# Starting bytes of SBUF tiles in a fused attention and gated feed-forward kernel: two unused stretches of 192 bytes

## The chip, the cores and the metric
One core of a Trainium2 chip runs the whole problem in one launch. The metric is the device time of that launch in microseconds, the median of several runs. The engines are named as in the profile: PE is TensorE's matmul, PEld its weight load, DVE is VectorE, ACT ScalarE, POOL GpSimd, and SP the queue that issues the DMAs.

## What is computed
```python
# batch 8, 12 heads, sequence 448, head dimension 64
scores = cap * np.tanh(q @ k.T / sqrt(64) / cap)
attn = softmax(scores)                      # exp, sum, divide
x = (attn @ v)                              # heads joined: 8 x 448 x 768
h = np.maximum(x @ w_in, 0.0)               # 768 -> 1024
u, v = h[..., :512], h[..., 512:]
v_n = (v - mean(v)) / np.sqrt(var(v) + 1e-06)
v_s = einsum('ts,bsd->btd', w_spatial, v_n) + b_spatial[None, :, None]
out = (u * v_s) @ w_out                     # 512 -> 768, float32
```

## The kernel before, in words
The kernel works through eight batches. For every batch three groups of four heads pass through attention: the scores (line 592, fp32, four 64 x 64 quadrants of the array, stationary and moving operand both from `raw`), tanh on ScalarE (line 596), exp on ScalarE (line 603), the product with the values (line 613, `v` stationary, the exponentials `tp` moving), and on VectorE folds over the exponentials for maximum and sum (line 631, tile `red`). The first three groups sum on TensorE instead, with a tile of ones (line 660, `one`). The normalised result is written as `xg`: a rounded high part of 448 columns, a low remainder of 448 columns, and a copy of some columns for one short block.

Then comes the mixture (the function `moe`), all in fp32r with operands split into a high and a low part, so that a product takes three matmuls: high by high, high by low, low by high. Its four products are
- u: lines 749 to 751, `wi1_h` or `wi1_l` stationary (128 columns of it), `xg` moving, 448 columns; 4 groups of 6 x 3 matmuls in a batch;
- v: lines 771 to 776, `xg` stationary, `wi2_h` or `wi2_l` moving, 512 columns; three groups of 6 x 3 and one of 6 x 2 in a batch;
- the spatial product: lines 840 to 845, `vh` or `vl` stationary, `ws_h` or `ws_l` moving, 448 columns; 4 groups of 11 in a batch;
- the output product: lines 865 to 867, `wo_h` or `wo_l` stationary, `xg` (now the gated product) moving, 448 columns; 6 groups of 4 x 3 in a batch.

A planner in the kernel orders all work beforehand: every task has an engine, a fixed cost and a key, and the planner plays the engines through and writes the instructions out in the order that it finds. The tiles' addresses don't enter it. Semaphore waits follow from the tiles that tasks share.

The tiles of SBUF lie one behind the other in each partition, in the order in which pools and tiles are made. Nearly all are a multiple of 256 bytes wide, so they keep the starting byte modulo 256 of what lies ahead of them. The exceptions before are `capt` (128 bytes), `one` (64 columns of use in a tile of 96, 384 bytes) and three tiles `lst` of 12 columns, which take 64 bytes each. So, modulo 256 bytes, there start
- at 0: `raw`, `wi2`, `ws`, `red`, `sh`, `st`, `wi1`, `wo`, `dt`, `one`;
- at 128, behind `one`: `v`, `tp`, `xf`, `rr`, `xg`, `u`, `stg`;
- at 64, behind the three `lst`: `vh`, `vl`, `o` and the staging tiles of the weights.

The slices that the matmuls read start at multiples of 256 bytes within their tiles, so an operand starts where its tile does.

Of the kernel before, what the change touches and what calls it, by code (L numbers as in the profile page):

```python
# [9 lines left out]
F32 = mybir.dt.float32  # L10
# [6 lines left out]
B, H, S, D = 8, 12, 448, 64  # L17
# [256 lines left out]
def attn_moe(ctx, tc, bounded, shared, qk, v, qk2, v2, cap, w_in, w_sp, w_out, out):  # L274
# [5 lines left out]
    def pool(name, bufs, space=None):  # L280
        kw = {"space": space} if space else {}
        return ctx.enter_context(tc.tile_pool(name=name, bufs=bufs, **kw))

    const = pool("const", 1)
# [27 lines left out]
    def weights(name, parts, width):  # L312
        return [const.tile([128, parts, width], F32R, name=f"{name}_{p}") for p in "hl"]
# [3 lines left out]
    if bounded:  # L317

        def keep(tag, n, width, fill=None):
            own[tag] = [const.tile([128, width], F32, name=f"{tag}{i}") for i in range(n)]  # L320
            for t in own[tag]:
                if fill is not None:
                    nc.gpsimd.memset(t, fill)

        keep("red", RED, 2 * PW)
        keep("sh", DEN, 64, 1.0)
        keep("st", DEN, 64, 1.0)
    wi1_h, wi1_l = weights("wi1", NP, FH)
    wo_h, wo_l = weights("wo", 4, DM)
    if bounded:  # L330
        keep("dt", DEN, 64, 1.0)
        one = const.tile([128, D + 32], F32, name="one")[:, :D]
        nc.gpsimd.memset(one, 1.0)

    if not bounded:
# [554 lines left out]
def either(ctx: ExitStack, tc: tile.TileContext, *args):  # L890
# [24 lines left out]
    with tc.If(bits <= CAP_BITS) as cmp:  # L915
        with ExitStack() as es:
            attn_moe(es, tc, True, shared, *args)
    with cmp.Else():
        with ExitStack() as es:
            attn_moe(es, tc, False, shared, *args)  # L920
# [29 lines left out]
```

## Time and profile before

| | |
|---|---|
| median of 3 runs | 736.54 us (735.54 to 736.76) |
| profiled execution, time | 735.65 us |
| profiled execution, span from first to last instruction | 733.8 us |
| granted TensorE clock, mean over the span | 0.992 |
| busy: TensorE, VectorE, ScalarE, GpSimd | 98%, 82%, 65%, 11% of the span |

The profile is of one execution. Its time lies 1.85 us above its span. TensorE's busy time counts a matmul from its start to a modelled end, and matmuls overlap in it, so the pace of a run of matmuls is read from the distances of their starts.

### The profile page before, as it was taken

To read this page: it belongs to the slowest core of one execution; us is meant where nothing else is said; L and a number is where in the kernel's file an instruction comes from. 1 tells how busy PE (TensorE), PEld (TensorE's weight loads), DVE (VectorE), ACT (ScalarE), POOL (GpSimd) and SP (SyncE) were. 2 spreads that over 40 slices of the span, in tenths; PEclk is the share of its full clock that TensorE was granted. 3 is DMA by queue.
4 is the path that set the end of the run, shared out by engine and by line. 5 is a ranking of instruction groups with operands and counts; after the bars stand their busy time and mean duration, and the time that the engine had idled before them with its cause. 6 is when DMAs were issued, how large, how long until landed. Compare 5 with 4: busy or idle time off the path is not lost.

```text
span 733.8 us, 12258 instructions
## 1 busy us (share of the span) xinstructions
PE 718.4 (98%) x4902; PEld 488.2 (67%) x4902; DVE 601.6 (82%) x849; ACT 480.0 (65%) x648; POOL 80.9 (11%) x71
## 2 busy tenths in 40 slices
PE   8996999999999999999999999999999999999997
PEld 3332676575668656786558688568565865698896
DVE  4899999999999989948999996299799688982520
ACT  6999657849784884649875833785876678324321
POOL 2234411600110001000120001000020000200100
PEclk9998999999999999999999999999999999999999
DMA  8565314424221441033330420213321131102002
GB/s 278 163 207 157 111 35 139 161 93 143 69 77 50 132 122 50 26 102 101 101 87 22 155 92 26 63 63 129 101 76 41 60 116 38 52 17 86 1 1 80
DMA packets 34263, 66.50 MB, mean 91 GB/s; under 512 B 6034, under 2 KB 21908, under 8 KB 34196
## 3 DMA queue, kind: packets, MB, share of 16 engines
q1 hardware_dynamic: 34196, 65.62, 28.1%
q8 instruction: 40, 0.66, 0.4%
q14 instruction: 27, 0.22, 0.1%
HBM read 54.40 MB, written 11.18 MB: 89 GB/s over the span
## 4 chain that ended last, share of the span: by engine, by line
PE 88%; DVE 5%; ACT 2%; DMA 2%; issue 1%; SPq 1%; POOL 0%; DVEq 0%; ACTq 0%
PE ps_s L592 15%; PE ps_x L613 15%; PE ps_acc L749 5%; PE ps_acc L750 5%; PE ps_acc L751 5%; PE ps_acc L865 5%; PE ps_acc L866 5%; PE ps_acc L867 5%; PE ps_acc L774 4%; PE ps_acc L776 4%; PE ps_acc L775 4%; PE ps_acc L843 2%; PE ps_acc L844 2%; PE ps_acc L845 2%; DVE red L631 2%; PE ps_acc L771 2%
## 5 line engine op out<-in xcount | busy, mean ns | idle before, releaser
L596 ACT ACTIVATE tp<-ps_s,capt 128x896 f32<-128x896 f32 x168 | 162.5, 1005 | 29.7 <-PE ps_s L592 22.2
L631 DVE TENSOR_TENSOR red<-red,tp 128x1792 f32<-128x1792 f32 x90 | 140.9, 1566 | 23.4 <-ACT tp L603 21.7
L603 ACT ACTIVATE tp<-tp,capt 128x1792 f32<-128x1792 f32 (+1 forms) x96 | 154.1, 1607 | 1.5
L592 PE MATMUL ps_s<-raw 64*64 64x448 f32 x1344 | 146.9, 545 | 3.5 <-ACT tp L596 3.3
L613 PE MATMUL ps_x<-tp,v 64*64 64x448 f32 x1344 | 140.0, 536 | 0.5 <-ACT tp L603 0.4
L631 DVE TENSOR_TENSOR red<-tp 128x1792 f32<-128x1792 f32 x45 | 91.2, 2027 | 13.8 <-ACT tp L603 12.9
L613 PEld LDWEIGHTS ps_x<-tp,v 64*64 64x64 f32 x1344 | 51.2, 133 | 75.9 <-issue 68.7
L592 PEld LDWEIGHTS ps_s<-raw 64*64 64x64 f32 x1344 | 47.4, 133 | 79.3 <-issue 47.5
L798 POOL TENSOR_TENSOR lst<-lst,capt 128x1 f32<-128x1 f32 x32 | 35.0, 1095 | 532.1 <-DVE lst L796 532.0
L749 PE MATMUL ps_acc<-xg,wi_h 128*128 128x448 f32 x180 | 67.5, 375 | 3.1 <-ACT xg L353 3.1
L750 PE MATMUL ps_acc<-xg,wi_h 128*128 128x448 f32 x180 | 66.8, 371 | 0.4 <-DVE xg L349 0.4
L751 PE MATMUL ps_acc<-xg,wi_l 128*128 128x448 f32 x180 | 66.4, 369 | 0.0
L865 PE MATMUL ps_acc<-xg,wo_h 128*128 128x448 f32 x176 | 65.1, 370 | 0.0
L866 PE MATMUL ps_acc<-xg,wo_h 128*128 128x448 f32 x176 | 64.5, 367 | 0.6 <-DVE xg L349 0.6
L867 PE MATMUL ps_acc<-xg,wo_l 128*128 128x448 f32 x176 | 64.4, 366 | 0.0
L353 ACT CAST xg<-o 128x448 fp32r<-128x448 f32 x32 | 18.1, 567 | 53.3 <-DVE o L850 47.8
L774 PE MATMUL ps_acc<-wi_h,xg 128*128 128x512 f32 x126 | 50.6, 402 | 0.0
L639 DVE STREAM_TRANSPOSE red<-red 128x896 f32<-128x896 f32 x45 | 49.6, 1102 | 0.7
L776 PE MATMUL ps_acc<-wi_h,xg 128*128 128x512 f32 x126 | 49.7, 395 | 0.0
L775 PE MATMUL ps_acc<-wi_l,xg 128*128 128x512 f32 x126 | 49.7, 394 | 0.0
L641 DVE TENSOR_REDUCE st<-red 128x28 f32<-128x896 f32 x45 | 48.6, 1079 | 0.7
L631 DVE TENSOR_TENSOR red<-red 128x896 f32<-128x896 f32 x45 | 48.6, 1081 | 0.6
(144 smaller groups left out, 1112.3 us busy)
## 6 DMA issues: line engine op xcount, KB each, us to landing
raw<-in_qk SPq DMA_DIRECT2D x48, 448.0 KB
rr<-rd SPq DMA_DIRECT2D x48, 224.0 KB
out<-o SPq DMA_DIRECT2D x48, 224.0 KB
w<-in_w_in SPq DMA_DIRECT2D x12, 512.0 KB
v<-in_v SPq DMA_DIRECT2D x24, 256.0 KB
v<-in_v SPq DMA_DIRECT2D x24, 192.0 KB
xg<-in_w_out SPq DMA_DIRECT2D x12, 256.0 KB
rd<-dt SPq DMA_DIRECT2D x48, 3.5 KB
```

The lines of the kernel that those rows point to most:

```text
L592: nc.tensor.matmul(ps.t[c * D:(c + 1) * D, e, :S], lhsT=f(raw[c].t)[r, k:k + D], rhs=f(raw[c].t)[r, :S], start=True, stop=True)
L596: th = add("A", act(PW, 1), kk("th", i), lambda ps=ps, tp=tp, o=o: nc.scalar.activation(out=tp.t[:, o:o + PW].rearrange("p (e q) -> p e q" ...
L603: ex = add("A", act_s(w, 1), kk("ex", i), lambda tp=tp, w=w: nc.scalar.activation(out=tp.t[:, :w], in_=tp.t[:, :w], func=AF.Exp, scale=ca) ...
L613: nc.tensor.matmul(x.t[e * D:(e + 1) * D, c, :S], lhsT=vts[g // 2].t[c * D:(c + 1) * D, (4 * (g % 2) + 2 * j + e) * D:(4 * (g % 2) + 2 * j ...
L631: nc.vector.tensor_tensor(o_(), i0(), i1(), op=op)
L749: nc.tensor.matmul(ps, lhsT=wi1_h[:, c, fs], rhs=x[:, XH:], start=(c == 0), stop=False)
L750: nc.tensor.matmul(ps, lhsT=wi1_h[:, c, fs], rhs=x[:, :S], start=False, stop=False)
L751: nc.tensor.matmul(ps, lhsT=wi1_l[:, c, fs], rhs=x[:, XH:], start=False, stop=(c == NP - 1))
L774: nc.tensor.matmul(ps, lhsT=x[:, XH:][:, ts], rhs=wi2_h[:, c], start=(c == 0), stop=False)
L865: nc.tensor.matmul(ps, lhsT=wo_h[:, c, ns], rhs=g[:, XH:], start=(c == 0), stop=False)
L866: nc.tensor.matmul(ps, lhsT=wo_h[:, c, ns], rhs=g[:, :S], start=False, stop=False)
L867: nc.tensor.matmul(ps, lhsT=wo_l[:, c, ns], rhs=g[:, XH:], start=False, stop=(c == 3))
```

## The change
It adds one tile of 48 columns (192 bytes) that nothing reads or writes, between the small tiles and the weights of the first product's u half, and it widens the unused part of the tile `one` from 32 columns to 80, which is 192 bytes more.

```diff
         keep("red", RED, 2 * PW)
         keep("sh", DEN, 64, 1.0)
         keep("st", DEN, 64, 1.0)
+    if bounded:
+        const.tile([128, 48], F32, name="gap")
     wi1_h, wi1_l = weights("wi1", NP, FH)
     wo_h, wo_l = weights("wo", 4, DM)
     if bounded:
         keep("dt", DEN, 64, 1.0)
-        one = const.tile([128, D + 32], F32, name="one")[:, :D]
+        one = const.tile([128, D + 80], F32, name="one")[:, :D]
         nc.gpsimd.memset(one, 1.0)
```

Modulo 256 bytes, `wi1`, `wo`, `dt` and `one` start at 192 afterwards, the tiles behind `one` at 0 (192 + 576 = 768), and `vh`, `vl`, `o` and the staging tiles at 192. `raw`, `wi2`, `ws`, `red`, `sh` and `st` stay at 0.

## Rows read from the trace of the kernel before

**Rows 1.** Page, part 1: busy us (share of the span) xinstructions
```profile
PE 718.4 (98%) x4902; PEld 488.2 (67%) x4902; DVE 601.6 (82%) x849; ACT 480.0 (65%) x648; POOL 80.9 (11%) x71
```

**Rows 2.** Page, part 4: the chain that ended last, by engine
```profile
PE 88%; DVE 5%; ACT 2%; DMA 2%; issue 1%; SPq 1%; POOL 0%; DVEq 0%; ACTq 0%
```

**Rows 3.** Two windows: start:end, length, each engine's busy us, clock, DMA, GB/s
```profile
62.00:77.04 15.04, 8.64 (x44) 4.60 (x37) 14.43 (x26) 14.36 (x24) 3.73 (x4) 0.66 0.50 163
77.04:728.64 651.60, 650.84 (x4302) 461.34 (x4300) 538.82 (x756) 410.69 (x566) 55.16 (x45) 1.00 0.25 78
```

**Rows 4.** Timeline of PE at granted clock 0.5: start us, us
```profile
74.34 0.57 PE L750 MATMUL ps_acc<-xg,wi_h 128*128 128x448 f32 x1
...
75.46 0.57 PE L750 MATMUL ps_acc<-xg,wi_h 128*128 128x448 f32 x1
```

**Rows 5.** Timeline, last batch: output product, then v, then u
```profile
660.22 0.36 PE L865 MATMUL ps_acc<-xg,wo_h 128*128 128x448 f32 x1
...
674.70 0.36 PE L867 MATMUL ps_acc<-xg,wo_l 128*128 128x448 f32 x1
674.89 0.39 PE L774 MATMUL ps_s<-wi_h,xg 128*128 128x512 f32 x1
...
690.00 0.40 PE L772 MATMUL ps_acc<-wi_l,xg 128*128 128x512 f32 x1
...
690.23 0.37 PE L749 MATMUL ps_acc<-xg,wi_h 128*128 128x448 f32 x1
690.23 0.19 PEld L750 LDWEIGHTS ps_acc<-xg,wi_h 128*128 128x128 f32 x1
```

**Rows 6.** Timeline, last batch: u, then the spatial product, then the output
```profile
709.14 0.36 PE L751 MATMUL ps_acc<-xg,wi_l 128*128 128x448 f32 x1
709.34 0.37 PE L843 MATMUL ps_s<-ws_h,vh 128*128 128x448 f32 x1
...
713.60 0.37 PE L841 MATMUL ps_s<-ws_h,vl 128*128 128x448 f32 x1
713.80 0.36 PE L865 MATMUL ps_x<-xg,wo_h 128*128 128x448 f32 x1
```

**Rows 7.** Lines by tile: duration ns min/median/max, first and last start
```profile
L867 PE MATMUL ps_acc<-xg,wo_l x176: 358/367/373, 148.1 to 720.9; 128*128 128x448 f32 x176
L775 PE MATMUL ps_acc<-wi_l,xg x126: 387/393/404, 90.9 to 627.0; 128*128 128x512 f32 x126
...
L844 PE MATMUL ps_acc<-ws_l,vh x87: 360/367/370, 106.2 to 704.9; 128*128 128x448 f32 x87
```

**Rows 8.** Timeline, first seam from u to the spatial product
```profile
122.61 0.36 PE L751 MATMUL ps_acc<-xg,wi_l 128*128 128x448 f32 x1
122.81 0.37 PE L843 MATMUL ps_acc<-ws_h,vh 128*128 128x448 f32 x1
```

**Rows 9.** Timeline, first seam from the spatial product to u
```profile
118.95 0.37 PE L841 MATMUL ps_acc<-ws_h,vl 128*128 128x448 f32 x1
119.15 0.36 PE L749 MATMUL ps_acc<-xg,wi_h 128*128 128x448 f32 x1
```

**Rows 10.** Timeline, first seam from v to u
```profile
196.29 0.40 PE L772 MATMUL ps_acc<-wi_l,xg 128*128 128x512 f32 x1
196.52 0.37 PE L749 MATMUL ps_acc<-xg,wi_h 128*128 128x448 f32 x1
```

**Rows 11.** Scores and value product by line: duration ns min/median/max
```profile
L592 PE MATMUL ps_s<-raw x1344: 536/536/971, 6.5 to 634.5; 64*64 64x448 f32 x192
...
L613 PE MATMUL ps_x<-tp,v x1344: 536/536/587, 13.8 to 639.7; 64*64 64x448 f32 x192
```

**Rows 12.** Groups by form on DVE: busy us, mean ns, idle before
```profile
L631 DVE TENSOR_TENSOR red<-tp 128x1792 f32<-128x1792 f32 x45 | 91.2, 2027 | 13.8 <-ACT tp L603 12.9
L631 DVE TENSOR_TENSOR red<-red,tp 128x1792 f32<-128x1792 f32 x45 | 90.9, 2020 | 15.2 <-ACT tp L603 14.7
```

**Rows 13.** Who waited for rr: us, times
```profile
  DVE xf L696: 0.4, 1
```

## Prediction

> **What bounds the kernel now.** I read the page's busy times first: TensorE is busy 98% of the span [rows 1]. The chain that ended last agrees: TensorE has 88% of it, VectorE 5%, DMA 2% [rows 2]. Two windows then tell where the other engines matter. From 62.00 to 77.04 us TensorE works 8.64 of 15.04 us while VectorE and ScalarE are busy almost throughout; from 77.04 to 728.64 it works 650.84 of 651.60 us [rows 3]. The granted clock is 1.00 in this second window and 0.66 in the first. So after 77 us TensorE's own stream alone sets the end, VectorE has 113 us to spare there, and a nanosecond per matmul is a nanosecond of the kernel times its count.
>
> Next I asked whether the matmuls themselves run at the pace of their columns, because after 77 us an address can move the end only through them. I counted from start to start. While the granted clock was 0.5, the fp32r matmuls of 448 columns started every 0.373 us (74.34 to 75.46 in three steps, [rows 4]), which is 448 columns at 1.2 GHz with nothing left over. At full speed the same columns would take 186.7 ns at 2.4 GHz, but a run of the output product takes 14.48 us for 71 intervals (660.22 to 674.70), 203.9 ns each [rows 5]. The product v with 512 columns (213.3 ns at 2.4 GHz) takes 15.11 us for 65 (674.89 to 690.00), 232.5 ns [rows 5]; the mean over all its runs is 232.6. The spatial product takes 4.26 us for 21 (709.34 to 713.60, [rows 6]); over its 322 intervals inside such runs the mean is 202.6 ns. The surplus over the columns is 17.2, 19.3 and 15.9 ns. By count of the loops there are 576 matmuls of the first product's u half and 576 of the output product (both 448 columns, call them u/o), 528 of v and 352 of the spatial product (g). The pot that an address could change is therefore 1152 x 17.2 + 528 x 19.3 + 352 x 15.9 = 19.8 + 10.2 + 5.6 = 35.6 us, 4.8% of the time.
>
> The surplus isn't even. In one line the lengths run from 358 to 373 ns in u/o, from 387 to 404 in v, from 360 to 370 in g [rows 7]; these ends are modelled and lie some 162 ns above the interval to the next start (the median 367 of L867 against 203.9). Within a run the intervals repeat in a short fixed cycle. So a state is carried from one matmul to the next, and a run settles into one of the cycles that its addresses allow.
>
> **The change part by part.** No instruction is added, removed or reordered: the order of work comes from the planner's fixed costs, and the two stretches hold no data. No queue, wait or transfer changes. What moves are starting bytes within a partition.
>
> I take the starting byte of the moving operand less that of the stationary operand loaded beside it, modulo 256. The load of the next weights starts with each matmul (both at 690.23, [rows 5]) and takes 0.19 us of its 0.20, so the two reads run together. From the tile sizes this difference is, before and after: u/o 128 (x at 128, wi1 and wo at 0), then 64 (x at 0, weights at 192); v 128 (wi2 at 0 moving, x at 128 stationary), then 0; g 192 (ws at 0, vh and vl at 64), then 64 (vh and vl at 192). The attention products keep theirs: scores read raw twice, and tp and v move together.
>
> The new differences 64 and 0 don't occur inside any run of before, but they occur at its seams, where one product hands over to the next.
> - Difference 64: last u matmul (x at 128) against the first g weights (vh at 64). 21 seams, 0.20 us at the first [rows 8] and at the last (709.14 to 709.34, [rows 6]), mean 203.1 ns.
> - Difference 0 with 448 columns: last g matmul (ws at 0) against wi1 or wo at 0. 22 seams, 0.20 us at the first [rows 9] and at the last (713.60 to 713.80, [rows 6]), mean 204.9 ns. Another kind, x moving against x stationary from u or o to v, has 6 seams, 0.19 us at the last (674.70 to 674.89, [rows 5]), mean 199.7.
> - Difference 0 with 512 columns: last v matmul (wi2 at 0) against wi1 at 0. 6 seams, 0.23 us at the first [rows 10] and at the last (690.00 to 690.23, [rows 5]), mean 232.5 ns.
>
> The sum: u/o 1152 x (203.1 - 203.9) = -0.9 us; v 528 x (232.5 - 232.6) = -0.1 us; g 352 x (203.1 - 202.6) = +0.2 us. Together about -0.8 us. A seam is one interval, entered from a state that another difference left, and a long run may settle elsewhere. The bounds from both sides are the shortest and longest lengths of each product [rows 7] held throughout, against the 366, 394 and 365 ns that belong to the mean intervals: u/o -8 to +7 ns, v -7 to +10, g -5 to +5, so -9.2 - 3.7 - 1.8 = -14.7 us and +8.1 + 5.3 + 1.8 = +15.2 us. I take the seam values, because the mean over states has stayed within 199.7 to 204.9 ns at 448 columns at all four differences, while the extremes are single members of a cycle. An uncertainty of 2 ns on u/o, 2 on v and 2 on g is 2.3, 1.1 and 0.7 us.
>
> The rest I cost at nothing. The absolute start seems to do nothing by itself: scores at byte 0 and the value product at byte 128 both have a median of 536 ns [rows 11]. VectorE's folds change from tp at 128 and red at 0 to both at 0; the first fold reads tp twice and the second red and tp, and they take 2027 and 2020 ns [rows 12], so 7 ns x 45 = 0.3 us bounds it, beside TensorE's work; without that cover it would be 0.3 us. The transfers land at other bytes (v and rr at 0 instead of 128), and VectorE waited for rr only 0.4 us, once [rows 13]; if that cover were gone, it would be that 0.4 us.
>
> [...]
>
> The profiled execution took 735.65 us, 0.89 below the median of the runs, 736.54; the sum applies to either: 734.9 and 735.7.
>
> **The rivals.** A difference of 0.2% is 1.47 us here, about what a measurement of this kernel can tell from no change.
>
> Faster: the collisions of u/o thin out at difference 64. It decides from -1.3 ns per u/o matmul (1.47 us / 1152) on. For it: g, already at another difference, is the fastest of the three at 202.6, and the shortest u/o lengths are 8 ns below the mean. Against: the 21 seams average only 0.8 ns less. Half the way to the shortest, -4 ns, gives -4.6 us and 731.9; all the way 727.3.
>
> Slower: in v, moving and stationary operands now start at the same byte, so each load begins in step with the stream that it runs beside, and v settles in its long intervals. It decides from +2.8 ns per v matmul (1.47 / 528); half the way to the longest, +5 ns, gives +2.6 us and 739.2, all the way 741.8. For it: the 22 seams with difference 0 are the slowest kind, 204.9. Against: the six with v's own width are at 232.5, and 199.7 was seen too.
>
> Nothing at all: only something finer than 64 bytes matters, and the time stays at 736.5. The lengths of u/o reach from 358 to 373 ns and those of g only from 360 to 370 [rows 7] at equal columns, which speaks against it; but the two products differ in more than their starts. [...]
>
> **How the numbers follow.** Little change by the sum above: 0.36, nothing at all 0.10, faster 0.32, slower 0.22. The first is likeliest: 735.7 us, with its own range of 735.1 to 738.0. For the range I go to the half-way prices on both sides, 731.9 and 739.2, and a little beyond for the settling that can't be read from seams: 731.5 to 740.0. That leaves about one in ten on either side. Faster by over 0.2% is 0.32, within it 0.46, slower 0.22.
>
> **What would show it.** In the changed kernel the same window from 77 us should still hold TensorE without gaps; the u/o runs should start every 203 ns, v's every 232 to 233, g's every 203, and the chain should be as before. If u/o runs fall below 201 the faster rival is right; if v runs rise above 236 the slower one. If all three cycles are unchanged to the nanosecond, 64 bytes don't matter. The prediction is wrong if seams don't stand for runs, if VectorE's folds change by more than 10 ns, or if the stretch before 77 us moves.

## The result, and the profile after

The changed kernel takes 728.75 us (median of 4 runs, 728.26 to 730.34) against 736.65 us of before in the same comparison: a ratio of 0.9898 with a 95% interval of 0.9878 to 0.9918, 1.0% faster. Forecast were 735.7 us and a range of 731.5 to 740.0; the measured time lies below both.

The page of the changed kernel, busy times and the chain by engine, to set beside [rows 1, 2]:

```profile
PE 711.1 (98%) x4902; PEld 486.6 (67%) x4902; DVE 600.7 (83%) x849; ACT 479.9 (66%) x648; POOL 80.3 (11%) x71
PE 85%; DVE 8%; ACT 2%; DMA 2%; issue 1%; SPq 1%; POOL 0%; DVEq 0%; ACTq 0%
```

TensorE's busy time is 7.3 us shorter with the same 4902 matmuls, the other engines' times change by at most 1.6 us, and the span (726.5 us) is 7.3 us shorter. The chain was forecast to stay as before and doesn't quite: TensorE has 85% of it instead of 88, VectorE 8% instead of 5. Windows of the changed kernel, cut at the corresponding instants (the columns of [rows 3]):

```profile
62.00:76.36 14.36, 8.08 (x39) 4.26 (x32) 13.74 (x25) 13.69 (x24) 3.23 (x4) 0.76 0.52 171
76.36:721.33 644.97, 644.04 (x4302) 460.68 (x4301) 537.94 (x757) 410.95 (x566) 55.20 (x45) 1.00 0.25 78
```

The second window held 651.60 us before and holds 644.97 now, with the same 4302 matmuls and hardly more idle time of TensorE (0.93 us, 0.76 before): 6.6 of the 7.3 us lie here, in the pace of the matmuls. The timeline of PE in the last batches, g, then the output product, then v, then u (start us, length us):

```profile
649.77 0.36 PE L845 MATMUL ps_acc<-ws_h,vh 128*128 128x448 f32 x1
...
653.98 0.36 PE L843 MATMUL ps_acc<-ws_h,vl 128*128 128x448 f32 x1
654.18 0.36 PE L867 MATMUL ps_acc<-xg,wo_h 128*128 128x448 f32 x1
...
668.38 0.36 PE L869 MATMUL ps_acc<-xg,wo_l 128*128 128x448 f32 x1
668.58 0.39 PE L776 MATMUL ps_s<-wi_h,xg 128*128 128x512 f32 x1
...
683.32 0.39 PE L774 MATMUL ps_acc<-wi_l,xg 128*128 128x512 f32 x1
683.54 0.36 PE L751 MATMUL ps_acc<-xg,wi_h 128*128 128x448 f32 x1
```

The 71 intervals of the output product take 14.20 us, 200.0 ns each, where [rows 5] had 14.48 us and 203.9; v's 65 take 14.74 us, 226.8 ns, where it had 15.11 and 232.5; g's 21 take 4.21 us, 200.5 ns, where [rows 6] had 4.26. Over all runs the means are 200.05 (u/o), 227.4 (v) and 200.6 ns (g), against 203.7, 232.6 and 202.6. (The 203.9 is the output product's; the u half had 203.5.) By the starts in the trace the intervals of the output product repeated 203, 212, 200, 209 and 196 ns before and repeat 202, 201 and 197 now: the run has settled into another cycle. The spread within a line has shrunk as well (duration ns min/median/max, as in [rows 7]):

```profile
L869 PE MATMUL ps_acc<-xg,wo_l x176: 360/362/368, 147.2 to 713.8; 128*128 128x448 f32 x176
L777 PE MATMUL ps_acc<-wi_l,xg x126: 389/389/402, 90.3 to 621.4; 128*128 128x512 f32 x126
L846 PE MATMUL ps_acc<-ws_l,vh x87: 360/360/367, 105.3 to 697.9; 128*128 128x448 f32 x87
```

So the shortest length didn't get shorter (358 before, 360 now; the ends are modelled); the long ones are gone. Between starts, the output product's intervals ran from 195 to 212 ns before and run from 197 to 206 now.

What VectorE and ScalarE do meanwhile doesn't set this pace. Two windows of the kernel before (the columns of [rows 3]) lie in runs of the output product:

```profile
155.00:163.00 8.00, 8.00 (x41) 7.36 (x40) 7.93 (x9) 4.98 (x6) 0.00 (x0) 1.00 0.25 92
714.00:728.00 14.00, 14.00 (x70) 12.89 (x69) 1.25 (x2) 3.23 (x6) 0.00 (x0) 1.00 0.20 76
```

VectorE is busy 7.93 of 8.00 us in the first and 1.25 of 14.00 in the second, ScalarE 4.98 and 3.23, and the two runs have 203.8 and 203.9 ns between starts. The DMA engines' share is much the same in both (0.25 and 0.20), so these windows say nothing of transfers.

What was costed at nothing stayed so. The attention products and VectorE's folds, from the lines' durations and the groups by form, beside [rows 11, 12]:

```profile
L594 PE MATMUL ps_s<-raw x1344: 536/536/951, 6.2 to 628.7; 64*64 64x448 f32 x192
...
L615 PE MATMUL ps_x<-tp,v x1344: 536/536/587, 13.5 to 634.0; 64*64 64x448 f32 x192
```

```profile
L633 DVE TENSOR_TENSOR red<-tp 128x1792 f32<-128x1792 f32 x45 | 91.2, 2027 | 13.2 <-ACT tp L605 12.3
L633 DVE TENSOR_TENSOR red<-red,tp 128x1792 f32<-128x1792 f32 x45 | 90.9, 2019 | 14.4 <-ACT tp L605 13.9
```

The starts account for the gain. From the 601st matmul (76.58 us before, 76.12 after) to the last, the intervals inside u/o runs sum to 3.94 us less, inside v runs to 2.62 less, inside g runs to 0.62 less, and where products or kinds of work change to 0.10 less; those inside the attention products sum to 0.43 more. That is 6.85 us, and the first 600 matmuls give 0.46. Most of the 0.43 us is one wait that the faster stream runs into: the timeline (in brackets the idle time and what ended it) shows the weight load of the scores waiting 0.90 us for ScalarE, where it waited 0.58 us before.

```profile
136.73 1.01 ACT L598 ACTIVATE tp<-ps_s,capt 128x896 f32<-128x896 f32 x1
...
137.79 0.21 PEld L594 LDWEIGHTS ps_s<-raw 64*64 64x64 f32 x8 [0.90 <-ACT tp L598]
```

The same load in the kernel before:

```profile
138.60 0.21 PEld L592 LDWEIGHTS ps_s<-raw 64*64 64x64 f32 x8 [0.58 <-ACT tp L596]
```

### The profile page after: what moved, and what is told of

Read it like the earlier page. It is cut to its first block, busy times and chain, and to the rows that moved or that the text cites. A ratio compares the mean times of both kernels' runs of the same rounds, so it can differ in the third digit from the quotient of the medians.

```text
span 726.5 us, 12258 instructions
## 1 busy us (share of the span) xinstructions
PE 711.1 (98%) x4902; PEld 486.6 (67%) x4902; DVE 600.7 (83%) x849; ACT 479.9 (66%) x648; POOL 80.3 (11%) x71
## 4 chain that ended last, share of the span: by engine, by line
PE 85%; DVE 8%; ACT 2%; DMA 2%; issue 1%; SPq 1%; POOL 0%; DVEq 0%; ACTq 0%
PE ps_s L594 14%; PE ps_x L615 14%; PE ps_acc L751 5%; PE ps_acc L867 5%; PE ps_acc L752 5%; PE ps_acc L868 5%; PE ps_acc L753 5%; PE ps_acc L869 5%; PE ps_acc L776 4%; PE ps_acc L777 4%; PE ps_acc L778 4%; DVE red L633 3%; PE ps_acc L845 2%; PE ps_acc L847 2%; PE ps_acc L846 2%; PE ps_acc L773 1%
## 5 line engine op out<-in xcount | busy, mean ns | idle before, releaser
L633 DVE TENSOR_TENSOR red<-tp 128x1792 f32<-128x1792 f32 x45 | 91.2, 2027 | 13.2 <-ACT tp L605 12.3
L751 PE MATMUL ps_acc<-xg,wi_h 128*128 128x448 f32 x180 | 66.9, 372 | 2.8 <-ACT xg L355 2.8
L752 PE MATMUL ps_acc<-xg,wi_h 128*128 128x448 f32 x180 | 65.7, 365 | 0.6 <-DVE xg L351 0.6
L633 DVE TENSOR_TENSOR red<-red 128x896 f32<-128x896 f32 x45 | 48.6, 1080 | 0.6
```

The costliest lines, as they stand in the source:

```text
L633: nc.vector.tensor_tensor(o_(), i0(), i1(), op=op)
L751: nc.tensor.matmul(ps, lhsT=wi1_h[:, c, fs], rhs=x[:, XH:], start=(c == 0), stop=False)
L752: nc.tensor.matmul(ps, lhsT=wi1_h[:, c, fs], rhs=x[:, :S], start=False, stop=False)
```

## The experiments

Two questions were put. Is it the difference between the two operands' starting bytes that sets a product's pace, or the byte at which one of them lies? And is the gain the sum of three separate terms? Every experiment changes only the sizes of unused stretches, so all kernels have the same instructions in the same order. The intervals are means over all runs of a product in one profiled execution (some 1080 for u/o, 505 for v, 322 for g). Single executions differ in the first 600 matmuls: in two profiles of the changed kernel the 601st matmul starts at 76.12 and 77.60 us. So paces are read from intervals, and the times carry intervals only where they were repeated. In the edits shown, the line `if bounded:` ahead of an added tile is left out, and `...` marks other lines left out.

**Both halves of the change by themselves.** The first has the gap alone, the second the wider tile alone:

```diff
+        const.tile([128, 48], F32, name="gap")
         one = const.tile([128, D + 32], F32, name="one")[:, :D]
```
```diff
-        one = const.tile([128, D + 32], F32, name="one")[:, :D]
+        one = const.tile([128, D + 80], F32, name="one")[:, :D]
```

> Only the tile of 192 unused bytes, the tile of ones as before. Starts modulo 256: wi1 and wo 192, x 64, vh and vl 0; moving less stationary: u/o 128 as before, v 192, spatial product 0. Relative theory (the difference within a product sets its pace): u/o runs at 203.9 ns as before, v and the spatial product at new values between 226 and 234 and between 200 and 205; time 733 to 738. Absolute theory (the byte at which x or the weights start sets it): u/o has no reason to come back to 203.9 and lies where the run with the pad alone lies or between 200 and 204.

> Only the wider tile of ones, no gap. Starts modulo 256: wi1 and wo 0, x 64, vh and vl 0; differences: u/o 64 as in the changed kernel, v 192, spatial product 0, these two as with the gap alone. Relative theory: u/o runs at 200.0 ns, v and the spatial product as with the gap alone, so the time is 1152 x 3.9 ns = 4.4 us below that of the gap alone. Absolute theory (x sets it): x is at 64 in both, so u/o and the time are equal.

The gap alone takes 737.22 us, a ratio to before of 1.0015 (1.0001 to 1.0029); the wider tile alone 733.31 us, 0.9961 (0.9945 to 0.9977). The timeline of PE in the kernel with the gap alone, output product and v:

```profile
662.35 0.36 PE L867 MATMUL ps_acc<-xg,wo_h 128*128 128x448 f32 x1
...
676.84 0.36 PE L869 MATMUL ps_acc<-xg,wo_l 128*128 128x448 f32 x1
677.03 0.39 PE L776 MATMUL ps_s<-wi_h,xg 128*128 128x512 f32 x1
...
692.20 0.40 PE L774 MATMUL ps_acc<-wi_l,xg 128*128 128x512 f32 x1
```

and in the kernel with the wider tile alone:

```profile
659.10 0.36 PE L865 MATMUL ps_acc<-xg,wo_h 128*128 128x448 f32 x1
...
673.30 0.36 PE L867 MATMUL ps_acc<-xg,wo_l 128*128 128x448 f32 x1
673.50 0.39 PE L774 MATMUL ps_s<-wi_h,xg 128*128 128x512 f32 x1
...
688.67 0.40 PE L772 MATMUL ps_acc<-wi_l,xg 128*128 128x512 f32 x1
```

In both x starts at byte 64. The 71 intervals of the output product take 14.49 us (204 ns) with the weights at 192 and 14.20 us (200 ns) with the weights at 0; v's 65 take 15.17 us in both. Over all runs u/o is at 203.8 and 200.2 ns, v at 233.3 and 233.4, g at 204.6 and 205.3. The absolute theory of x wanted equal u/o; it is out. Nor does the byte of the weights alone set it: they lie at 0 in the kernel before and in the one with the wider tile, which have 203.7 and 200.2 ns. The medians are 3.9 us apart, where 1152 x 3.6 ns = 4.1 us. The gap alone leaves u/o where it was and moves v and g to differences that cost more: 1.2 us more than before by the intervals, 1.1 by the medians. The wider tile alone takes u/o down and the same two up: 2.6 us less by the intervals, 2.8 by the medians.

**One product at a time.** Moving only wi1 and wo, with the small tiles dt and one behind them, to 64 gives u/o the difference 64 and leaves v and g:

```diff
+        const.tile([128, 16], F32, name="gap")
-        one = const.tile([128, D + 32], F32, name="one")[:, :D]
+        one = const.tile([128, D + 16], F32, name="one")[:, :D]
```

> Only wi1, wo, dt and the ones move, to 64; x stays at 128, vh and vl at 64. Differences: u/o 64, v 128 and spatial product 192 as before. Relative theory: u/o at 200.0 ns, v at 232.6, spatial at 202.6; the time is 1152 x 3.9 ns = 4.4 us below before, 732.2. Absolute theory: x hasn't moved and the weights are not at 192, so nothing changes: 736.6.

Measured 732.88 us, a ratio of 0.9949 (0.9932 to 0.9965), u/o 200.05, v 232.7, g 202.8 ns. The output product in its timeline:

```profile
658.19 0.36 PE L867 MATMUL ps_acc<-xg,wo_h 128*128 128x448 f32 x1
...
672.39 0.36 PE L869 MATMUL ps_acc<-xg,wo_l 128*128 128x448 f32 x1
```

Again 14.20 us, at a third pair of bytes (x 128, weights 64). Moving only wi2, to 128, gives v the difference 0 while x stays at 128:

```diff
+        const.tile([128, 32], F32, name="gap")
     wi2_h, wi2_l = weights("wi2", NP, FH)
+        const.tile([128, 32], F32, name="gap2")
```

> Only wi2 moves, from 0 to 128, so that v has difference 0; all else starts where it did before. Relative theory with additive terms: u/o 203.9 and spatial 202.6 as before, v 227.4 instead of 232.6, 528 x 5.2 = 2.7 us less than before: 733.4 to 734. Rival that x at byte 0 is what made v faster: no change, 736.2.

Measured 733.94 us, 0.9966 (0.9954 to 0.9979), u/o 203.8, v 227.5, g 202.65 ns. Its v run takes 14.75 us for 65:

```profile
673.81 0.40 PE L778 MATMUL ps_s<-wi_h,xg 128*128 128x512 f32 x1
...
688.56 0.40 PE L776 MATMUL ps_acc<-wi_l,xg 128*128 128x512 f32 x1
```

The two medians lie 3.2 and 2.1 us below the 736.08 and 736.02 us of before beside them; the terms by interval are 1152 x 3.65 = 4.2 and 2.7. The intervals came out as forecast, the times gained somewhat less. In the profiled executions the two take 3.98 and 2.22 us less than before from the 601st matmul to the last; with the 0.62 us of g that makes 6.82, against 6.85 in the changed kernel, so the terms add up there. In these single executions the rest lies ahead of the 601st matmul, which starts at 77.73 and 77.39 us, and at 76.58 before.

**x at 0, weights at 0.** Only the tile of ones is changed, to 512 bytes:

```diff
-        one = const.tile([128, D + 32], F32, name="one")[:, :D]
+        one = const.tile([128, D + 64], F32, name="one")[:, :D]
```

> No gap, the tile of ones 512 bytes: wi1 and wo at 0, x at 0, vh and vl at 192. Differences: u/o 0, v 0 and spatial product 64 as in the changed kernel. Relative theory: v at 227.4 and spatial at 200.6 give 2.7 + 0.7 = 3.4 us less than before; u/o at a new value, from seams 199.7 to 204.9. Absolute theory (x at 0 is what helps): all three as in the changed kernel, 728.8.

Measured 732.37 us, 0.9948 (0.9935 to 0.9962), u/o 203.3, v 227.6, g 200.6 ns.

```profile
658.62 0.37 PE L865 MATMUL ps_acc<-xg,wo_h 128*128 128x448 f32 x1
...
673.01 0.36 PE L867 MATMUL ps_acc<-xg,wo_l 128*128 128x448 f32 x1
673.22 0.39 PE L774 MATMUL ps_s<-wi_h,xg 128*128 128x512 f32 x1
...
687.98 0.39 PE L772 MATMUL ps_acc<-wi_l,xg 128*128 128x512 f32 x1
```

x at 0 isn't what helps u/o: 14.39 us here against 14.20. v and g are as in the changed kernel, since their differences are.

**Other differences, and two exchanged.** Three kernels have an unused stretch ahead of ws as well (56, 32 and 56 columns), then 48, 48 and no columns ahead of wi1, and a tile of ones with 8, 40 and 48 unused columns:

```diff
+        const.tile([128, 56], F32, name="gap_ws")
     ws_h, ws_l = weights("ws", 4, S)
...
+        const.tile([128, 48], F32, name="gap")
-        one = const.tile([128, D + 32], F32, name="one")[:, :D]
+        one = const.tile([128, D + 8], F32, name="one")[:, :D]
```

> Starts modulo 256: ws 224, wi1 and wo 160, x 192, vh and vl 128; differences u/o 32, v 64, spatial product 96, none tried yet. Theory of the difference modulo 256 in steps of 64 or coarser (only multiples of 64 tell): u/o at 32 gives the 203.2 of difference 0 or the 200.0 of 64, the spatial product at 96 the 200.6 of 64 or the 203.9 of 128. Finer theory: values of their own. v at 64: the single seams with it gave 226.2 in the changed kernel.

> Starts: ws 128, wi1 and wo 64, x 224, vh and vl 160; differences u/o 160, v 32, spatial product 224. Step-of-64 theory: u/o at 203.9 (128) or 202.6 (192), spatial at 202.6 (192) or 203 to 205 (0), v between 226 and 228 if 0 and 64 are alike. Finer theory: values of their own, outside these pairs.

> Starts: ws, wi1 and wo 224, x 160, vh and vl 96; differences u/o 192, v 96, spatial product 128: the two that u/o and the spatial product had in the kernel before, exchanged, at other bytes. Relative theory: u/o at 202.6 and the spatial product at 203.9, since only columns and difference count. Rival (each product has its own dependence): u/o at 192 and the spatial product at 128 lie elsewhere by 1 ns or more.

One execution each: 737.22, 733.81 and 735.88 us, beside 736.18 of before. At 32 u/o is at 205.6 ns, worse than at either neighbour (203.3 at 0, 200.0 at 64), and v at 64 is at 229.3, between (227.6 at 0, 232.7 at 128):

```profile
661.25 0.36 PE L869 MATMUL ps_acc<-xg,wo_h 128*128 128x448 f32 x1
...
675.91 0.37 PE L871 MATMUL ps_acc<-xg,wo_l 128*128 128x448 f32 x1
676.12 0.40 PE L778 MATMUL ps_s<-wi_h,xg 128*128 128x512 f32 x1
...
691.01 0.39 PE L776 MATMUL ps_acc<-wi_l,xg 128*128 128x512 f32 x1
```

(14.66 us for 71, 14.89 for 65.) So 32 bytes tell, and the step-of-64 theory is out. The second of the three has u/o at 160 with a mean of 201.5 ns, and g at 224 with 204.35; there, runs of one kernel settle differently. This one is at 14.20 us for 71 intervals, and others of the same kernel average 206.5 ns:

```profile
658.86 0.36 PE L869 MATMUL ps_acc<-xg,wo_h 128*128 128x448 f32 x1
...
673.06 0.36 PE L871 MATMUL ps_acc<-xg,wo_l 128*128 128x448 f32 x1
```

In the third, u/o has g's old difference 192 and g has u/o's old 128. u/o is at 202.4 and g at 204.4 ns; forecast were 202.6 and 203.9. The first is met, the second is half a nanosecond off, which stays unexplained (g's runs of 22 matmuls average 204.6 ns, those of 11 204.3). The rival theory, that each product has a dependence of its own, asked for 1 ns or more.

```profile
656.22 0.36 PE L845 MATMUL ps_acc<-ws_h,vh 128*128 128x448 f32 x1
...
660.51 0.37 PE L843 MATMUL ps_acc<-ws_h,vl 128*128 128x448 f32 x1
660.72 0.37 PE L867 MATMUL ps_acc<-xg,wo_h 128*128 128x448 f32 x1
...
675.08 0.36 PE L869 MATMUL ps_acc<-xg,wo_l 128*128 128x448 f32 x1
```

**Which weights: those loaded beside, or a matmul's own?** In the u half wi1_l is put 64 bytes behind wi1_h, and the tile of ones takes 256 bytes:

```diff
+            if bounded and name == "wi1" and p == "l":
+                const.tile([128, 16], F32, name="gap")
...
-        one = const.tile([128, D + 32], F32, name="one")[:, :D]
+        one = const.tile([128, D + 0], F32, name="one")[:, :D]
```

> Inside the u half the two weight tiles get unequal differences: wi1_h 64, wi1_l 0. The three matmuls of a triple are x high by wi1_h, x low by wi1_h, x high by wi1_l. Theory that the weights loaded beside a matmul count: the second matmul, beside which wi1_l is loaded, starts a longer or shorter interval than in a run at 64, and the first and third have the loads of difference 64. Theory that a matmul's own weights count: it is the third. Output product all at 0: 203.1 by the relative theory. v at 192 and spatial product at 0 as with the gap alone: 233.3 and 204.6.

One execution, 736.19 us. The intervals behind the first, second and third matmul of a triple average 201.7, 202.4 and 202.5 ns: they lie within 0.8 ns and none stands out. A state carried along would smear whatever one of them causes; that is the author's supposition, and no run shows it. This doesn't tell the two theories apart, and it stays open. The output product, all at difference 0, is at 204.3 ns, 1.2 above the 203.1 of the output product in the kernel with x and weights at 0. In both kernels its long runs settle either near 202.6 or near 206.5 ns, and only the mixture differs.

**A better version?** u/o and g keep 64, v gets the two differences that were left, 160 and 224:

```diff
+        const.tile([128, 24], F32, name="gap_ws")      # 8 for v at 224
     ws_h, ws_l = weights("ws", 4, S)
...
+        const.tile([128, 48], F32, name="gap")
-        one = const.tile([128, D + 32], F32, name="one")[:, :D]
+        one = const.tile([128, D + 16], F32, name="one")[:, :D]
```

> Starts: ws 96, wi1 and wo 32, x 96, vh and vl 32. Differences u/o 64 and spatial product 64 as in the changed kernel, with every byte another; v 160, not tried yet. Relative theory: u/o 200.0 and spatial 200.6 again; the time is that of the changed kernel plus 528 times what v has above 227.4: with 227 it is 728.8, with 233 731.7. Absolute theory: u/o away from 200.0 by 1 ns or more.

> Starts: ws 32, wi1 and wo 224, x 32, vh and vl 224. Differences u/o 64, spatial product 64, v 224, not tried yet. Relative theory: u/o 200.0 and spatial 200.6; v between 226 and 234, the time 728 to 732.

> The changed kernel again, beside the others on one chip: 728.5 to 729.5, u/o 200.0, v 227.4, spatial product 200.6.

Measured on one chip: v at 160 gives 732.04 us (ratio 0.9936, 0.9919 to 0.9953), v at 224 gives 732.02 (0.9938, 0.9921 to 0.9956), the changed kernel 728.76 (0.9894, 0.9877 to 0.9910). u/o is at 200.05, 200.1 and 200.0 ns in the three, g at 200.5, 200.8 and 200.5, although no tile of these products starts at the same byte in any two of them; v is at 234.2, 233.2 and 227.3. The first of the three:

```profile
658.03 0.36 PE L869 MATMUL ps_acc<-xg,wo_h 128*128 128x448 f32 x1
...
672.22 0.36 PE L871 MATMUL ps_acc<-xg,wo_l 128*128 128x448 f32 x1
672.43 0.40 PE L778 MATMUL ps_s<-wi_h,xg 128*128 128x512 f32 x1
...
687.65 0.39 PE L776 MATMUL ps_acc<-wi_l,xg 128*128 128x512 f32 x1
```

The output product keeps its 14.19 us and v takes 15.22 us for 65. v's 5.9 to 6.9 ns above the changed kernel, times 528, are 3.1 to 3.6 us; the medians are 3.3 us apart. No version tried beats the changed kernel.

All means together, moving less stationary start modulo 256 bytes, ns between starts:

| difference | 448 columns, u/o | 448 columns, g | 512 columns, v |
|---|---|---|---|
| 0 | 203.3, 204.3 | 203.9 to 205.3 | 227.3 to 227.6 |
| 32 | 205.6 | | 233.3 |
| 64 | 200.0 to 200.2 | 200.5 to 200.8 | 229.3 |
| 96 | | 205.35 | 233.5 |
| 128 | 203.7 to 203.8 | 204.4 | 232.6, 232.7 |
| 160 | 201.5 | | 234.2 |
| 192 | 202.4 | 202.6 to 202.8 | 233.3, 233.4 |
| 224 | | 204.35 | 233.2 |

## Why the prediction was wrong

The place was right: after 77 us the pace of TensorE's matmuls sets the end, and the difference between the two starts moves it: at difference 64 u/o is at 200.0 to 200.2 ns at five pairs of bytes, and with x at byte 64 in both it is at 203.8 ns with the weights at 192 and at 200.2 with the weights at 0. The surplus over the columns is the author's estimate from [rows 4]: 448 columns in 373.3 ns at granted clock 0.5 give its 1.2 GHz, twice that the 2.4, half of the 373.3 its 186.7 ns, and 512/448 of that v's 213.3. That nothing was left over at clock 0.5 is part of this estimate, and no matmul of 512 columns runs at that clock in the profile of either kernel, so the figure for v was not measured.

The step that failed is "I take the seam values". It put the single intervals at the seams of before in the place of whole runs: -0.8 ns for u/o, -0.1 for v, +0.5 for g. The runs gave -3.65, -5.2 and -2.0. In time: -0.9, -0.1 and +0.2 us against 1152 x 3.65 = 4.2, 528 x 5.2 = 2.7 and 352 x 2.0 = 0.7 us less. (The prediction set the output product's 203.9 for all of u/o, whose mean was 203.7; that is 0.2 us.) A seam is one interval that follows a run at another difference, and a run settles into a cycle of its own: at difference 64 the seams of before average 203.1 ns and the runs of the changed kernel 200.0. What a matmul hands on to the next no run shows; what the traces show is the order of the intervals. In the changed kernel's v, at difference 0, a run can start with intervals such as 236, 228, 233 and 231 ns before it repeats 227, 227 and 226, and one of only 11 matmuls averages 232.7. The prediction named this caution and then gave it 2 ns of uncertainty for each product: 4.1 us if all fall together, where 6.8 were needed. Nor did these uncertainties enter the likeliest branch: its range of 735.1 to 738.0 is 736.54 us plus or minus 0.2%. "The prediction is wrong if seams don't stand for runs" is what came true.

The faster rival had the right sign, place and almost the size for u/o: half the way to the shortest length, -4 ns, against -3.65 measured, and the u/o runs did fall below 201. It had only u/o in it, and so ended at 731.9. That the other full price, 727.3, lies near the measured time is chance: it has u/o fall by 8 ns and leaves v and g alone. The slower rival was wrong in its direction: with both operands at the same byte v settled at 227.4 ns and gave a third of the gain. It rested on the 22 seams of 448 columns at difference 0, which say nothing of 512 columns. The low end of the range was set by the faster rival alone; a case in which all three products settle lower at once wasn't priced, though the bound of -14.7 us from the shortest lengths held it.

That nothing would happen is refuted by the gap alone against the wider tile alone. Moving only wi1 and wo, with dt and one, changed the u/o interval from 203.7 to 200.05 ns, so where the weights lie in relation to x does tell. Why it tells wasn't shown: the collisions of which the faster rival speaks are the author's supposition, and the traces show only starts and intervals. All starts here are multiples of 32 bytes, and the intervals differ by up to 7 ns at equal columns (200.0 to 205.6 for 448 in u/o, 227.3 to 234.2 for 512).

The costs put at nothing were right: attention at 536 ns, the folds at 2027 and 2019 ns. That a nanosecond per matmul is a nanosecond of the kernel held nearly: 7.6 us by the terms, 7.4 between the two profiled executions, with 0.43 us handed back inside the attention products and 0.46 gained ahead of the 601st matmul, where two profiles of one kernel differ by more than that.

## What to carry to other kernels

Where long runs of matmuls set the end (here fp32r, with 448 and 512 columns; nothing else was tried), and the trace has a stretch at a lower granted clock, compare the interval between their starts with the one from there, scaled by the clock; if it lies several per cent higher (here 203.9 ns against half of 373.3, 9%), the distance between the moving and the stationary tile modulo 256 bytes is worth a few padded variants, product by product, since the terms add up (here 6.82 us one by one, 6.85 together). Price such a change by runs and not by single intervals at a hand-over: a run settles into a cycle that its entry doesn't show (here 200.0 ns against seams of 203.1). Where several terms have an unknown sign, price the case in which they fall the same way before drawing the range.

## What the runs showed of the hardware that had not been expected

At granted clock 1.00 the fp32r matmuls of this kernel cost 200.0 to 205.6 ns for 448 columns and 227.3 to 234.2 for 512, by the difference of the two starts modulo 256 bytes and by little else that was varied. That 256 bytes more change nothing can be seen at difference 64: with a tile of ones of 320 bytes or of 576, which puts x 256 bytes further from the weights, u/o stays at 200.0 to 200.2 ns. The dependence isn't monotone and doesn't carry over from one width to the other: at 448 columns 64 is the best that was tried and 32 and 96 the worst, at 512 columns 0 is the best by 2 ns and 64 the second. Bytes finer than 32 apart weren't tried. At one difference several cycles can occur in one kernel: at 160 the runs of u/o average 200.0 or 206.5 ns, at 0 mostly 202.6 or 206.5. A mean in the table is then a mixture. What makes an interval longer, and whether the weights loaded beside a matmul count or its own, wasn't settled. At the granted clock 0.5 the u matmuls start every 373.3 ns in the kernel before, at difference 128 [rows 4], and in the changed kernel, at difference 64 (73.13 to 75.74 us in seven steps).
